# Seven block products in place of eight for the second layer's first product

## The chip, the cores and the metric

The kernel runs on one core of a Trainium2 chip. Times are device microseconds (us) of one execution. Engines go by their names in the profile: PE is TensorE's matmul stream and PEld its weight loads, DVE is VectorE, ACT is ScalarE, SP is SyncE, which here only issues DMAs. The program gives each engine its own list of instructions, in an order fixed when it is built.

## The reference

Sliding-window attention (4 sequences of 576 tokens, 8 heads of 64, window 64) gives x of 2304 tokens by 512. Two gated layers follow, each with a w_in of 512 by 2048 and a w_out of 2048 by 512:

```python
attn = softmax(where(mask, q @ k.T / 8, -1e9)); x = attn @ v      # 2304 x 512
h = x @ w_in1;  x = (h - tanh(h)) @ w_out1
h = x @ w_in2;  out = (h * sigmoid(1.702 * h)) @ w_out2
```

The four weights arrive as 64-bit floats and are converted on the chip.

## The kernel before

**Numbers.** Every operand of a large product is kept as two float32r tiles, a rounded high part and the rest (ACT copies `hi`, DVE subtracts `lo`). `three` (L540 to L545) makes one product of three matmuls: hi*hi, hi*lo, lo*hi. So a product of 128 by 128 weights with 512 tokens is three matmuls of 512 columns.

**Layers.** The 2048 hidden features are 16 groups f of 128. A step of a block of n tokens is `hid` (12 matmuls into one PSUM bank psh, 4 slices kk of the 512 inputs), then `act1` (ACT, L567 or L569), `act2` (DVE, L573), `act3` (ACT, L577), `act4` (DVE, L581), and two steps later `proj`, which adds to the accumulator banks acc. Layer 1 (blocks of 512, 512, 256, 512, 512 tokens) sends its result to DRAM (`xs`, L636), layer 2 (512, 512, 512, 512, 256) loads it back (`load_x2`). Blocks 0 and 1 of layer 1 are made in two parts each, which layer 2 adds (L664). The attention of tokens 1024 to 2303 runs in between layer 1's steps.

**Weights.** `plan_w` loads one group of 128 (512 KB), then ACT takes the absolute value (L275), four DVE operations form the 32-bit number (L279, L282, L288, L294), ACT rounds the high part (L301), DVE takes the rest (L306). A converted pair (w_in and w_out of one f) lives in one of 16 SBUF tiles, tags w0 to w15. Layer 2's pair f takes the tile of layer 1's pair f once that has had its last use (`last_proj[f]`).

**Order.** `Plan` is a list scheduler that runs when the program is built. Each task has the engines it may use with a planned time, a due time as its priority, what it comes after, and buffers that it takes (`acq`) and gives back (`rel`), out of fixed counts: raw=3, cw=2, s=4, psh=2, gp=3 and so on. It yields one order for PE, DVE, ACT and SP. PE's large products are chained in a fixed order. The planned times are constants, for instance 0.62 for a DVE operation on 512 elements and 0.36 on 256.

## Time and profile before

| what | value |
|---|---|
| median of 3 runs | 888.97 us (888.82 to 889.29) |
| profiled execution, its own time | 886.63 us |
| its span, first to last instruction | 884.8 us |
| mean granted TensorE clock | 0.994 of full |
| PE, PEld, DVE, ACT busy | 863.4, 725.9, 470.6, 374.7 us |
| DMA bytes | 72.93 MB |

The span is 1.83 us under the profiled execution's own time, and that time is 2.34 us under the median of the runs without a profile. Layer 2 begins at 482 us of the span.

### The profile page before, as it was taken

The numbers are of one execution on the slowest core, as the hardware profiler recorded it, in microseconds if no ns is written. First come the engines' busy times: TensorE is split into PE (matmuls) and PEld (weight loads), VectorE is DVE, ScalarE is ACT, GpSimd is POOL, SyncE is SP. The second block draws the span as 40 slices with busy tenths as digits, with TensorE's granted clock in tenths as the row PEclk, the third lists the DMA queues.
The fourth block names the chain that finished last, engine by engine and source line by source line (L and its number), as shares of the span: only waits on it lengthen the run. The fifth ranks groups of instructions, "written<-read, shape, count | busy, mean of one in ns | idle before, by whom it ended". The sixth has DMA issues, their size and how long they took to land.

```text
span 884.8 us, 13040 instructions
## 1 busy us (share of the span) xinstructions
PE 863.4 (98%) x5188; PEld 725.9 (82%) x5188; DVE 470.6 (53%) x867; ACT 374.7 (42%) x888; POOL 4.0 (0%) x19
## 2 busy tenths in 40 slices
PE   6799999999999999999999999999999999999998
PEld 5588888888899888878888888888888888888897
DVE  6899999233555325445999995233323332322232
ACT  6878565223546325543556653222222222222222
POOL 1000000000000000000000000000000000000000
PEclk8999999999999999999999999999999999999999
DMA  9645454111132102101554551020002000200000
GB/s 335 237 123 170 144 191 159 32 48 54 61 120 90 49 0 84 54 25 72 167 192 143 191 165 49 0 96 1 1 0 96 1 1 0 72 1 1 34 15 24
DMA packets 44205, 72.93 MB, mean 82 GB/s; under 512 B 3312, under 2 KB 24304, under 8 KB 44144
## 3 DMA queue, kind: packets, MB, share of 16 engines
q1 hardware_dynamic: 43712, 71.58, 24.1%
q8 instruction: 40, 0.66, 0.3%
q10 hardware_dynamic: 432, 0.52, 0.2%
q14 instruction: 21, 0.17, 0.1%
HBM read 60.56 MB, written 11.53 MB: 81 GB/s over the span
## 4 chain that ended last, share of the span: by engine, by line
PE 93%; DMA 2%; DVE 2%; ACT 1%; SPq 0%; issue 0%; ACTq 0%
PE acc L545 45%; PE psh L545 44%; PE psa L419 2%; PE psa L484 1%; PE psa L467 1%; DMA raw<-in_w_in 1%; ACT s L444 1%; DMA early<-in_k 1%; DMA early<-in_v 1%; DVE xl L504 0%; DVE nm L432 0%; DVE s L460 0%; DVE cw L288 0%; DVE w L306 0%; ACT s L472 0%
## 5 line engine op out<-in xcount | busy, mean ns | idle before, releaser
L545 PE MATMUL psh<-xh,w 128*128 128x512 f32 (+1 forms) x1312 | 391.3, 365 | 3.2 <-DVE g L573 2.5
L545 PEld LDWEIGHTS psh<-xh,w 128*128 128x128 f32 x1312 | 238.7, 189 | 44.1 <-DVE g L573 2.7
L573 DVE TENSOR_TENSOR g<-psh,g 128x512 f32<-128x512 f32 (+1 forms) x164 | 102.4, 624 | 286.8 <-ACT g L569 196.2
L545 PE MATMUL psh<-xl,w 128*128 128x512 f32 (+1 forms) x656 | 238.5, 364 | 0.2 <-DVE xl L504 0.2
L545 PE MATMUL acc<-gh,w 128*128 128x512 f32 (+1 forms) x672 | 198.4, 362 | 0.0
L545 PE MATMUL acc<-w,gh 128*128 128x512 f32 x576 | 190.3, 389 | 0.0
L545 PEld LDWEIGHTS psh<-xl,w 128*128 128x128 f32 x656 | 123.7, 189 | 20.0 <-DVE xl L504 0.5
L545 PEld LDWEIGHTS acc<-gh,w 128*128 128x128 f32 x672 | 122.1, 190 | 20.7 <-issue 1.5
L581 DVE TENSOR_TENSOR gl<-g,gh 128x512 fp32r<-128x512 f32 (+1 forms) x164 | 102.5, 625 | 66.3 <-ACT gh L577 65.0
L569 ACT ACTIVATE g<-psh 128x512 f32<-128x512 f32 (+1 forms) x80 | 44.5, 556 | 207.2 <-PE psh L545 207.0
L577 ACT ACTIVATE gh<-g 128x512 fp32r<-128x512 f32 (+1 forms) x164 | 95.4, 582 | 80.7 <-DVE g L573 80.5
L545 PEld LDWEIGHTS acc<-w,gh 128*128 128x128 f32 x576 | 108.2, 188 | 22.1
L545 PE MATMUL acc<-gl,w 128*128 128x512 f32 (+1 forms) x336 | 120.9, 360 | 0.0
L545 PE MATMUL acc<-w,gl 128*128 128x512 f32 x288 | 112.2, 390 | 0.0
L567 ACT ACTIVATE g<-psh 128x512 f32<-128x512 f32 (+1 forms) x84 | 45.0, 538 | 127.8 <-PE psh L545 127.8
L545 PEld LDWEIGHTS acc<-gl,w 128*128 128x128 f32 x336 | 63.8, 190 | 9.2
L545 PEld LDWEIGHTS acc<-w,gl 128*128 128x128 f32 x288 | 54.1, 188 | 10.7
L275 ACT ACTIVATE cw<-raw 128x512 f32<-128x512 f32 x64 | 43.6, 681 | 21.5 <-DVE w L306 17.0
L301 ACT ACTIVATE w<-cw 128x512 fp32r<-128x512 f32 x64 | 40.7, 637 | 24.7 <-DVE cw L294 24.4
L288 DVE SCALAR_TENSOR_TENSOR cw<-raw,cw 128x512 uint32<-128x512 uint32 x64 | 43.9, 686 | 1.0
L306 DVE TENSOR_TENSOR w<-cw,w 128x512 fp32r<-128x512 f32 x64 | 43.8, 684 | 0.7 <-ACT w L301 0.7
L294 DVE SCALAR_TENSOR_TENSOR cw<-raw,cw 128x512 uint32<-128x512 uint32 x64 | 43.8, 685 | 0.2
(58 smaller groups left out, 458.6 us busy)
## 6 DMA issues: line engine op xcount, KB each, us to landing
raw<-in_w_in SPq DMA_DIRECT2D x32, 512.0 KB, 3.7
raw<-in_w_out SPq DMA_DIRECT2D x32, 512.0 KB, 3.5
vt<-in_v SPq DMA_DIRECT2D x11, 512.0 KB, 3.6
xs<-os SPq DMA_DIRECT2D x20, 256.0 KB, 3.2
out<-os SPq DMA_DIRECT2D x16, 256.0 KB, 2.2
kt<-in_k SPq DMA_DIRECT2D x9, 384.0 KB, 4.1
qt<-in_q SPq DMA_DIRECT2D x11, 256.0 KB, 2.8
early<-in_v SPq DMA_DIRECT2D x5, 512.0 KB, 8.0
```

Source lines behind the costliest of these rows:

```text
L275: nc.scalar.activation(bits[key].bitcast(F32), raw[key].bitcast(F32)[:, :, 1], AF.Abs)
L288: nc.vector.scalar_tensor_tensor(out=bits[key], in0=raw[key][:, :, 0], scalar=29, in1=bits[key], op0=ALU.logical_shift_right, op1=ALU.bitw ...
L294: nc.vector.scalar_tensor_tensor(out=bits[key], in0=raw[key][:, :, 1], scalar=0xC0000000, in1=bits[key], op0=ALU.bitwise_and, op1=ALU.bitw ...
L301: nc.scalar.activation(wt[layer, f][:, i, 0, :], bits[key].bitcast(F32), AF.Copy)
L306: nc.vector.tensor_tensor(out=lo, in0=bits[key].bitcast(F32), in1=hi.bitcast(F32), op=ALU.subtract)
L419: nc.tensor.matmul(ps[h][part(j, h), p, :], lhsT=qt[j][r, p, :], rhs=kt[j][r, :, p, :], start=not on_pe, stop=not on_pe or p == NP - 1,)
L545: nc.tensor.matmul(ps, lhsT=a, rhs=b, start=first and i == 0, stop=last and i == 2)
L567: nc.scalar.activation(g, psh[s], AF.Tanh)
L569: nc.scalar.activation(g, psh[s], AF.Sigmoid, scale=BETA)
L573: nc.vector.tensor_tensor(out=g, in0=psh[s], in1=g, op=ALU.subtract if s[0][0] == 1 else ALU.mult)
L577: nc.scalar.activation(gh, g, AF.Copy)
L581: nc.vector.tensor_tensor(out=gl, in0=g, in1=gh.bitcast(F32), op=ALU.subtract)
```

## The change

Layer 2's blocks become one of 256 tokens (tokens 0 to 255, computed as before) and two units of 1024 tokens. In a unit, h is computed pair by pair: pair j holds the feature groups 2j and 2j+1. Both matrices are cut in two by two blocks (features by inputs: A11, A12, A21, A22, each 128 by 256; inputs by tokens: B11 and so on, each 256 by 512), and the four blocks of h come from seven products of 6 matmuls each (Winograd's form), with sums ahead and behind:

- `plan_wd` (8 times, among layer 1's steps, one for each pair): converts the two w_in groups, forms S1 to S4 on DVE, splits the eight blocks in hi and lo and stores them in DRAM (`wd`, 2 MiB for each pair).
- `stream`/`load_ws`: load a pair's blocks from `wd` into four tiles (tags w8 to w11, 1 MiB each): four blocks for the first 256 tokens, seven for a unit.
- w_out of layer 2 now lives two groups to a tile in w0 to w7 and is gated behind the last store of `wd`.
- `plan_xu`: loads the unit's x from `xs`, forms T1 to T4 on DVE and splits B11, T1, B22, T3, T2, B21, T4 in hi and lo, in two halves i that share their buffers (kq, v). T1, T3, B21, B22 of unit 0 take the tiles w12 to w15 after layer 1's `last_proj` of 12 to 15.
- `Ma`, `Mb`: four products, then three; between and behind them stand two `proj` fillers of 12 matmuls. DVE forms U, W, V, C22, C11, C12, C21 out of PSUM. The gated blocks of the first 512 tokens go to `proj` at once, those of the second 512 to DRAM (`u_store`) and come back (`u_back`) for 16 `proj` behind the eighth pair.
- `UB`: in unit 0 the products use the banks h, h, a0, a1 and the accumulators acc0 to acc3, in unit 1 the other way round.
- The kernel's last step is now a `proj` of two groups on four token tiles, each evicted in halves.

```diff
+    sizes = {1: [512, 512, 256, 512, 512], 2: [256]}
     blocks = {l: [(sum(z[:i]), n) for i, n in enumerate(z)] for l, z in sizes.items()}
-    NB1, NB2 = len(blocks[1]), len(blocks[2])
+    NB1 = len(blocks[1])
+    units = [256, 1280]
...
-    plan = Plan(dict(raw=3, cw=K["cw"], s=K["s"], psh=2, g=2, gp=3, kq=1, v=1, sa=K["sa"], x=2, acc0=1, acc1=1, acc2=1, acc3=1, a0=1, a1=1))
+    plan = Plan(dict(raw=3, cw=K["cw"], s=K["s"], psh=2, g=2, gp=3, kq=1, v=1, sa=K["sa"], x=2, acc0=1, acc1=1, acc2=1, acc3=1, a0=1, a1=1, ws=4))
...
+    A21, A11, A12, A22, S1, S2, S3, S4 = range(8)
+    HB = NB // 2
+    wd = {}
+    stage = {}
+    def blocks_of(j):
+        a, b = (bits[2, 2 * j + i, 0].bitcast(F32) for i in range(2))
...
+        for o, a, b, op in ((S1, A21, A22, ALU.add), (S2, S1, A11, ALU.subtract), (S3, A11, A21, ALU.subtract), (S4, A12, S2, ALU.subtract)):
+            nc.vector.tensor_tensor(out=x[o], in0=x[a], in1=x[b], op=op)
+    def wd_hi(j, i):
+        o = stage[j, i] = st.tile([P, NB], F32R, tag="s", name="wds")
+        nc.scalar.activation(o[:, :HB], blocks_of(j)[i], AF.Copy)
+    def wd_lo(j, i):
+        o = stage[j, i]
+        nc.vector.tensor_tensor(out=o[:, HB:], in0=blocks_of(j)[i], in1=o[:, :HB].bitcast(F32), op=ALU.subtract)
+    def wd_store(j, i):
+        if j not in wd:
+            wd[j] = dr.tile([P, 8, NB], F32, name=f"wd{j}")
+        nc.sync.dma_start(out=wd[j][:, i], in_=stage.pop((j, i)).bitcast(F32))
+    wd_done = {}
+    def plan_wd(j, d, after):
+        signs, ls, cs = [], [], []
+        both = add({"SP": 1.2}, lambda _: [load_w((2, 2 * j + i, 0)) for i in range(2)], d - 5, after, acq=("raw", "raw"), size=2 * P * NB * 8)
+        for i in range(2):
+            key = (2, 2 * j + i, 0)
+            def go(e, fn, t, *a, key=key, **kw):
+                return add({e: t}, lambda _: fn(key), d + 3 * i, *a, **kw)
+            l = both
+            c = absol = go("ACT", conv_abs, 0.56, [l] + cs, acq=() if i else ("cw", "cw"))
+            for fn, x in ((conv_clamp, 0.36), (conv_mant, 0.36), (conv_low, 0.62)):
+                c = go("DVE", fn, x, [c])
+            signs.append(go("DVE", conv_sign, 0.62, [c], rel=[("raw", l)] if i else []))
+            ls.append(l)
+            cs.append(absol)
+        sums = add({"DVE": 1.4}, lambda _: wd_sums(j), d + 6, signs)
+        los, sts = [], []
+        for i in range(8):
+            h = add({"ACT": 0.32}, lambda _, i=i: wd_hi(j, i), d + 6 + i, [sums], acq=("s",))
+            los.append(add({"DVE": 0.36}, lambda _, i=i: wd_lo(j, i), d + 6 + i, [h]))
+            sts.append(add({"SP": 0.6}, lambda _, i=i: wd_store(j, i), d + 6 + i, [los[-1]], rel=[("s", h)], size=P * NB * 4))
+        wd_done[j] = sts
+        add({"none": 0.0}, lambda _: None, d, los, rel=[("cw", cs[0]), ("cw", cs[0]), ("raw", ls[0])])
+        return sts[-1]
...
+    def load_ws(key, j, a, b):
+        n = count[0] = count[0] + 1
+        t = wp.tile([P, 4, NB], F32R, tag=f"w{8 + (n - 1) % NS}", name="ws")
+        wstream[key] = (t, a)
+        nc.sync.dma_start(out=t[:, : b - a].bitcast(F32), in_=wd[j][:, a:b])
...
+    UB = [(["h", "h", "a0", "a1"], ["acc0", "acc1", "acc2", "acc3"]), (["acc0", "acc1", "acc2", "acc3"], ["h", "h", "a0", "a1"])]
...
+    def load_u(u, what, i, kk, t0):
+        for c, b, z in pieces(t0, NB):
+            nc.sync.dma_start(out=full(u, what, i)[:, c], in_=xs[b, parts[b][0]][:, kk, z])
+    def load_u_more(u, what, i, kk, c, b, z, fa):
+        t = x2[u, what, i, b] = st.tile([P, NB], F32, tag="s", name="x2b")
+        nc.sync.dma_start(out=t[:, c], in_=xs[b, fa][:, kk, z])
...
+    def combine(u, o, a, b, op, i):
+        o, a, b = (full(u, w, i) for w in (o, a, b))
+        nc.vector.tensor_tensor(out=o, in0=a, in1=b, op=op)
...
+    def prod(u, j, n, a, b):
+        key = (1 + u, j, 0 if a < S2 else 1)
+        ah, al = ws_of(key, a)
+        bh, bl = x_space(u, b)
+        for i in range(2):
+            c = slice(i * P, (i + 1) * P)
+            three(mb[u, j, n], ah[:, c], al[:, c], bh[i], bl[i], i == 0, i == 1)
+    def m_open(u, j):
+        mb[u, j, 0] = bank(UB[u][0][0], "m")
+        prod(u, j, 0, A11, "B11")
+    def m_first(u, j):
+        for n, a, b in ((1, S2, "T2"), (2, S1, "T1"), (3, S3, "T3")):
+            mb[u, j, n] = bank(UB[u][0][n], "m")
+            prod(u, j, n, a, b)
+    def m_more(u, j, n, a, b):
+        mb[u, j, n] = bank(UB[u][0][n], "m")
+        prod(u, j, n, a, b)
...
+    def u_one(u, j):
+        r = cv.tile([P, 2, NB], F32, tag="raw", name="uv")
+        ut[u, j, 0], ut[u, j, 1] = r[:, 0], r[:, 1]
+        nc.scalar.activation(ut[u, j, 0], mb[u, j, 0], AF.Copy)
+    def u_add(u, j, o, a, n):
+        if o == "W":
+            ut[u, j, 2] = st.tile([P, NB], F32, tag="cw", name="c12", bufs=K["cw"])
+        if o == "C22":
+            ut[u, j, 3] = st.tile([P, NB], F32, tag="s", name="c22")
+        nc.vector.tensor_tensor(out=u_val(u, j, o), in0=u_val(u, j, a), in1=mb[u, j, n], op=ALU.add)
...
+    def u_proj(u, t, fs, es):
+        for e in es:
+            if fs[0] == 0:
+                uacc[u, t, e] = bank(UB[u][1 - t][e], "uacc")
+            for f in fs:
+                wh, wl = w_outof(2, f)
+                _, gh, gl = ug[u, t, f]
+                c = slice(e * P, (e + 1) * P)
+                three(uacc[u, t, e], wh, wl, gh[:, c], gl[:, c], f == 0, f == KF - 1, swap=True)
...
+        if what == "h" and layer == 2:
+            plan_w((2, f, 1), due["p", s] - 6, [last_proj[f // 2]], wd_done[NJ - 1])
+            if f % 2 == 0:
+                j = f // 2
+                stream((0, j), j, 0, 4, d)
...
+    def stream(key, j, a, b, d):
+        n = len(streams)
+        last = list(streams.values())[-1:]
+        after = wd_done[j] + last + ([last_proj[8 + n]] if n < NS else [])
+        streams[key] = add({"SP": 0.6}, lambda _: load_ws(key, j, a, b), d - 14, after, acq=("ws",), size=P * (b - a) * NB * 4)
...
+    for what, s in seq:
+        layer, f = s[0][0], s[1]
+        if layer == 2 and not wd_done:
+            last = None
+            for j in range(NJ):
+                d = K["wd"][0] + K["wd"][1] * j
+                near = [made[x] for x in made if due["h", x] < d - 8]
+                last = plan_wd(j, d + K["wd"][2], near[-1:] + [last])
+        if layer == 1 or what == "h" or f < KF - 2:
+            plan_step(what, s)
...
+    def plan_xu(u, d, ends_of, gate):
+        done = []
+        t4own = xown = last = None
+        for i in range(2):
+            srcs = {}
+            acq, before = ("kq", "v"), [last]
+            lfirst = None
+            for n, (what, kk, t) in enumerate((("B11", i, 0), ("B12", i, 1), ("B22", 2 + i, 1), ("B21", 2 + i, 0))):
+                dd = d - 30 + 12 * i + 2 * n
+                t0 = units[u] + t * NB
+                deps = [stored[z, kk] for c, b, _ in pieces(t0, NB) for z in turns if z[:2] == (1, b)]
+                near = [made[s] for s in made if due["h", s] < dd - K["xu"]]
+                np_ = len(list(pieces(t0, NB)))
+                c = l = add(
+                    {"SP": 0.6 * np_}, lambda _, a=(u, what, i, kk, t0): load_u(*a), dd - 6,
+                    deps + near[-1:] + gate + [lfirst], acq=() if lfirst else acq, size=P * NB * 4,
+                )
+                lfirst = lfirst or l
+                for sl, b, z in pieces(t0, NB):
+                    for fa in parts[b][1:]:
+                        m = add({"SP": 0.6}, lambda _, a=(u, what, i, kk, sl, b, z, fa): load_u_more(*a), dd - 5.9, [l], acq=("s",), size=P * NB * 2)
+                        c = add({"DVE": 0.36}, lambda _, a=(u, what, i, sl, b): add_u(*a), dd, [c, m], rel=[("s", m)])
+                srcs[what] = c
+            dd = d - 20 + 12 * i
+            los = {}
+            def split(what, *w, acq=(), i=i, dd=dd, los=los):
+                h = add({"ACT": 0.54}, lambda _: u_hi(u, what, i), dd, list(w) + ends_of(what), acq=acq)
+                los[what] = add({"DVE": 0.62}, lambda _: u_lo(u, what, i), dd, [h])
+                return h
+            def comb(o, x, y, op, *w, i=i, dd=dd):
+                return add({"DVE": 0.62}, lambda _: combine(u, o, x, y, op, i), dd, list(w))
+            h = split("B11", srcs["B11"], xown, acq=("x",) if i == 0 else ())
+            xown = xown or h
+            t1 = comb("T1", "B12", "B11", ALU.subtract, srcs["B12"], srcs["B11"])
+            split("T1", t1)
+            t3 = comb("T3", "B22", "T3", ALU.subtract, srcs["B22"], t1)
+            split("B22", srcs["B22"])
+            split("T3", t3)
+            t2 = comb("T2", "T3", "T2", ALU.add, t3, t1, los["B11"])
+            split("T2", t2)
+            split("B21", srcs["B21"])
+            t4 = comb("T4", "T4", "T2", ALU.subtract, t2, los["B21"])
+            h = split("T4", t4, t4own, acq=("sa", "sa") if i == 0 else ())
+            t4own = t4own or h
+            last = add({"none": 0.0}, lambda _: None, dd, list(los.values()), rel=[("kq", lfirst), ("v", lfirst)])
+            done += los.values()
+        return done, xown, t4own
...
+    rest = [("p0", s) for s in last_p0]
+    order = []
+    for u in range(2):
+        for j in range(NJ):
+            order += [("Ma", u, j), rest.pop(0) if rest else None, ("Mb", u, j), rest.pop(0) if rest else None]
+            rest += [("p", u, 0, (2 * j + i,)) for i in range(2)]
+        q_ = [("p", u, 1, (f,)) for f in range(KF)]
+        order += [rest.pop(0), q_[0], rest.pop(0)]
+        if u == 0:
+            order += q_[1 : KF - 2]
+            rest = q_[KF - 2 :]
+        else:
+            order += q_[1 : KF - 2] + [("p", u, 1, (KF - 2, KF - 1))]
+    order = [o for o in order if o]
...
+    had = {0: lambda w: [last_proj[KF - 4 + ("T1", "T3", "B21", "B22").index(w)]] if w in ("T1", "T3", "B21", "B22") else []}
...
+            stream((1 + u, j, 0), j, 1, 5, d)
+            stream((1 + u, j, 1), j, 5, 8, d)
+            mk = keys(UB[u][0])
+            a0 = prev = add({"PE": MS}, lambda _, u=u, j=j: m_open(u, j), d, [prev, streams[1 + u, j, 0]] + (xdone if j == 0 else []), acq=mk[:1])
+            a1 = prev = add({"PE": 3 * MS}, lambda _, u=u, j=j: m_first(u, j), d + MS, [prev, streams[1 + u, j, 1]], acq=mk[1:])
+            chain += [a0, a1]
+            def sm(o_, a, n, *w, u=u, j=j, d=d, **kw):
+                return add({"DVE": 0.7}, lambda _: u_add(u, j, o_, a, n), d + 4, list(w), **kw)
+            p1 = add({"ACT": 0.52}, lambda _, u=u, j=j: u_one(u, j), d + 2, [a0], acq=("raw",))
+            uu = sm("U", "P1", 1, p1, a1, rel=[(mk[1], a1)])
+            ww = sm("W", "U", 2, uu, acq=("cw",))
+            vv = sm("V", "U", 3, ww)
+            c22 = sm("C22", "W", 3, ww, vv, acq=("s",))
+            up[u, j] = (a0, a1, p1, uu, ww, vv, c22, mk)
...
+            for n, a, x, w in ((0, A12, "B21", [p1]), (2, S4, "B22", [ww]), (3, A22, "T4", [vv, c22])):
+                rel = [("ws", streams[1 + u, j, i]) for i in ((1,) if n == 2 else (0,) if n == 3 else ())]
+                if end and n == 3:
+                    rel += [("x", uo[u][0]), ("sa", uo[u][1]), ("sa", uo[u][1])]
+                b = prev = add({"PE": MS}, lambda _, a=(u, j, n, a, x): m_more(*a), d, [prev] + w, rel=rel)
+                ms.append(b)
+                chain.append(b)
+            if end:
+                gone[u] = b
...
+            y22 = act("C22", c22, d)
+            c11 = sm("C11", "P1", 0, d + 3, a0, uu, ms[0])
+            y11 = act("C11", c11, d + 3)
+            c12 = sm("C12", "W", 2, d + 3.5, a1, c22, ms[1])
+            c21 = sm("C21", "V", 3, d + 3.6, a1, c22, ms[2])
+            y21 = act("C21", c21, d + 4)
+            y12 = act("C12", c12, d + 5)
+            s22 = add({"SP": 0.6}, lambda _, u=u, j=j: u_store(u, j, "C22"), d + 5, [y22], rel=[("s", c22)], size=P * NB * 4)
+            s12 = add({"SP": 0.6}, lambda _, u=u, j=j: u_store(u, j, "C12"), d + 5, [y12], rel=[("cw", ww)], size=P * NB * 4)
+            store_of[u, 2 * j], store_of[u, 2 * j + 1] = s12, s22
+            los = []
+            for f, y in ((2 * j, y11), (2 * j + 1, y21)):
+                h = add({"ACT": 0.54}, lambda _, u=u, f=f: g_hi(u, 0, f), d + 5, [y], acq=("gp",))
+                gates[u, 0, f] = add({"DVE": 0.62}, lambda _, u=u, f=f: g_lo(u, 0, f), d + 5, [h])
+                los.append(gates[u, 0, f])
+                owner[u, 0, f] = h
...
+                    bk = add({"SP": 0.6}, lambda _, u=u, f=f: u_back(u, f), d - 9, [store_of[u, f]] + chain[-6:-5], acq=("raw",), size=P * NB * 4)
+                    h = add({"ACT": 0.54}, lambda _, u=u, f=f: g_hi(u, 1, f), d - 4, [bk] + (chain[-3 + i : -2 + i or None] if f > 1 else [gates[u, 0, KF - 2 + f]]), acq=("gp",))
+                    gates[u, 1, f] = add({"DVE": 0.62}, lambda _, u=u, f=f: g_lo(u, 1, f), d - 4, [h], rel=[("raw", bk)])
+                    owner[u, 1, f] = h
...
+            es = [[0], [1, 2, 3]] if fs[0] == 0 else [[0], [1], [2], [3]] if final else [[0, 1, 2, 3]]
+            for z in es:
+                last_e = z[-1] == 3
+                p = prev = add(
+                    {"PE": MS / 2 * len(z) * len(fs)}, lambda _, a=(u, t_, fs, z): u_proj(*a), d, [prev] + need,
+                    acq=[bk_[e] for e in z] if fs[0] == 0 else (), rel=[("gp", owner[u, t_, f]) for f in fs] if last_e else (),
+                )
```

## Rows read from the trace of the kernel before

**Rows 1.** The page's first part: busy us, share of the span, instructions.
```profile
PE 863.4 (98%) x5188; PEld 725.9 (82%) x5188; DVE 470.6 (53%) x867; ACT 374.7 (42%) x888; POOL 4.0 (0%) x19
```
**Rows 2.** The waits of PE, 100 to 840 us: total, times, longest.
```profile
PE psh L545 <- ACT xh L499: 0.7, 1, 0.7
PE psa L484 <- DVE s L474: 0.3, 1, 0.3
PE psh L545 <- DVE xl L504: 0.2, 1, 0.2
```
**Rows 3.** The chain that ended last, layer 2's first steps: start, us, what.
```profile
482.13 2.72 PE psh L545 x12
484.85 2.72 PE acc L545 x12
```
**Rows 4.** The same chain at the end of the kernel (256-token steps, tail).
```profile
873.92 1.39 PE acc L545 x6
875.31 1.43 PE psh L545 x12
876.75 4.12 PE acc L545 x18
```
**Rows 5.** Groups by form: busy us, mean ns of one, idle before.
```profile
L545 PEld LDWEIGHTS psh<-xh,w 128*128 128x128 f32 x1312 | 238.7, 189 | 44.1 <-DVE g L573 2.7 <-issue 1.0 <-ACT xh L499 0.8
L573 DVE TENSOR_TENSOR g<-psh,g 128x512 f32<-128x512 f32 x124 | 85.7, 691 | 249.0 <-ACT g L569 171.0 <-ACT g L567 77.3
L577 ACT ACTIVATE gh<-g 128x512 fp32r<-128x512 f32 x124 | 78.4, 632 | 68.4 <-DVE g L573 68.2
L288 DVE SCALAR_TENSOR_TENSOR cw<-raw,cw 128x512 uint32<-128x512 uint32 x64 | 43.9, 686 | 1.0
L294 DVE SCALAR_TENSOR_TENSOR cw<-raw,cw 128x512 uint32<-128x512 uint32 x64 | 43.8, 685 | 0.2
L306 DVE TENSOR_TENSOR w<-cw,w 128x512 fp32r<-128x512 f32 x64 | 43.8, 684 | 0.7 <-ACT w L301 0.7
L275 ACT ACTIVATE cw<-raw 128x512 f32<-128x512 f32 x64 | 43.6, 681 | 21.5 <-DVE w L306 17.0 <-DMA raw<-in_w_in 2.9 <-ACT gh L577 0.8
L569 ACT ACTIVATE g<-psh 128x512 f32<-128x512 f32 x64 | 38.3, 598 | 180.7 <-PE psh L545 180.6
L282 DVE TENSOR_SCALAR cw<-cw 128x512 uint32<-128x512 uint32 x64 | 26.9, 422 | 0.4
L577 ACT ACTIVATE gh<-g 128x256 fp32r<-128x256 f32 x40 | 17.0, 426 | 12.3 <-DVE g L573 12.3
L581 DVE TENSOR_TENSOR gl<-g,gh 128x256 fp32r<-128x256 f32 x40 | 16.9, 422 | 13.2 <-ACT gh L577 12.7 <-PE acc L545 0.5
```
**Rows 6.** Stretches: PE, PEld, DVE, ACT, POOL busy (instructions), clock, DMA share, GB/s.
```profile
160.00:200.00 40.00, 40.00 (x179) 33.10 (x177) 11.69 (x18) 10.22 (x17) 0.00 (x0) 1.00 0.08 27
200.00:240.00 40.00, 40.00 (x303) 32.94 (x302) 17.24 (x30) 17.42 (x55) 0.00 (x0) 1.00 0.17 60
240.00:295.00 55.00, 55.00 (x604) 52.79 (x603) 29.07 (x61) 29.58 (x102) 0.00 (x0) 1.00 0.30 97
295.00:345.00 50.00, 50.00 (x290) 41.51 (x289) 17.48 (x29) 17.39 (x42) 0.00 (x0) 1.00 0.08 24
345.00:395.00 50.00, 48.67 (x383) 38.92 (x381) 24.78 (x42) 25.14 (x80) 0.00 (x0) 1.00 0.19 59
395.00:406.00 11.00, 11.00 (x48) 9.12 (x49) 2.71 (x5) 3.12 (x6) 0.00 (x0) 1.00 0.00 1
406.00:482.00 76.00, 76.00 (x337) 62.90 (x337) 69.25 (x128) 41.03 (x69) 0.00 (x0) 1.00 0.47 159
...
571.00:837.00 266.00, 266.00 (x1186) 220.70 (x1186) 77.52 (x117) 68.73 (x118) 0.00 (x0) 1.00 0.07 22
```
**Rows 7.** Stretches of the kernel's first part, same columns.
```profile
60.00:80.00 20.00, 17.93 (x249) 15.50 (x248) 18.76 (x43) 15.08 (x57) 0.00 (x0) 1.00 0.54 176
100.00:150.00 50.00, 50.00 (x222) 41.39 (x222) 48.85 (x92) 29.72 (x49) 0.00 (x0) 1.00 0.51 170
```
**Rows 8.** L279 (a conversion's first DVE step) alone, 395 to 482 us.
```profile
395.00:482.00 87.00, 7.49 (x18) 1.00 0.41 139
```
**Rows 9.** DMA issues: KB each, median us to landing.
```profile
xs<-os SPq DMA_DIRECT2D x20, 256.0 KB, 3.2
x<-xs SPq DMA_DIRECT2D x8, 256.0 KB, 4.0
x2b<-xs SPq DMA_DIRECT2D x8, 256.0 KB, 4.3
```
**Rows 10.** The first 20 us of the span, columns as in rows 6.
```profile
0.00:20.00 20.00, 12.98 (x164) 9.74 (x166) 13.44 (x33) 13.19 (x49) 4.00 (x19) 0.87 0.94 327
```

More of the change, by code (lines that the diff above doesn't have):

```diff
@@ L107, in order @@
                     for k, owner in t["rel"]:
-                        at(end + self.HOP, "back", (k, owner["own"][k]))
+                        at(end + self.HOP, "back", (k, owner["own"][k].pop(0)))
                     for o in t["outs"]:
@@ L145 @@
     fill=0.75,
+    xu=34.0,
+    wd=(190.0, 25.0, 60.0),
     seg=(4, 7),
@@ L590, in proj @@
         _, gh, gl = gt.pop(s)
-        wh, wl = (wt[layer, f][:, 1, j, :] for j in range(2))
+        wh, wl = w_outof(layer, f)
         n = c1 - c0
@@ new lines, in attn_moe2_kernel, with full @@
+    xtmp = {}
+    IN_PLACE = dict(B12="T3", B11="T2", B21="T4")
+    def full(u, what, i):
+        if (u, i) not in xtmp:
+            k_, v_ = (ap_.tile([P, 2, NB], F32, tag=t, name="xt", bufs=1) for t in "kv")
+            q_ = ap_.tile([P, NB], F32, tag="q", name="xt", bufs=1)
+            xtmp[u, i] = dict(T2=k_[:, 0], T3=k_[:, 1], T1=v_[:, 0], B22=v_[:, 1], T4=q_)
+        return xtmp[u, i][IN_PLACE.get(what, what)]
+    def load_u(u, what, i, kk, t0):
+        for c, b, z in pieces(t0, NB):
+            nc.sync.dma_start(out=full(u, what, i)[:, c], in_=xs[b, parts[b][0]][:, kk, z])
@@ L770, in attn_moe2_kernel, with plan_step @@
     x2_planned = set()
-    w2_planned = set()
-    for what, s in seq:
+    chain = []
+    def plan_step(what, s):
+        nonlocal prev
         z, f = s
@@ L779, in attn_moe2_kernel @@
             plan_x2(bi, d)
-        if layer == 2 and (f, 0) not in w2_planned:
-            for i in range(2):
-                w2_planned.add((f, i))
-                plan_w((2, f, i), due["hp"[i], s] - 6, [last_proj[f]])
+        if what == "h" and layer == 2:
[3 more added lines that the diff above has]
+                stream((0, j), j, 0, 4, d)
         if what == "h":
```

235 lines of the change are left out of this document (196 added, 39 removed).

## The prediction

> **What bounds the kernel now.** I read the page's busy times first. PE is busy 98% of the span, DVE 53%, ACT 42% [rows 1]. Since an average can hide a stage with another limit, the next view is PE's waits behind the first 100 us: three waits, 1.2 us in all, up to 840 us [rows 2]. The idle PE time left over lies in the first 80 us and in the tail, which the change doesn't touch. Third is the chain of waits in layer 2: it is matmuls alone, `hid` and `proj` in turn, each 2.72 us for 12 matmuls of 512 columns [rows 3], so one matmul costs 2.72/12 = 0.2267 us. That this is the pace of the matmuls and not of what feeds them shows in two rows: a weight load lasts 0.189 us [rows 5], less than 0.2267, and with half the columns 12 matmuls of `hid` take 1.43 us, 0.119 each, with a weight load for each as before [rows 4]. Hence every matmul taken out of layer 2 gives back 0.2267 us, as long as what replaces it stays under PE.
>
> **What is removed.** Before, four blocks of 512 tokens take 4 x 16 x 12 = 768 matmuls of `hid`. After, two units take 2 x 8 pairs x 7 products x 6 = 672. The difference is 96, that is 8 groups of 12: 8 x 2.72 = 21.76 us. `proj` keeps its number (768 and 96), and the 256-token block only moves from the end to the front of layer 2. A product ends after 6 matmuls and then changes its bank; `proj` in layer 2 changes banks after every 3 and still takes 2.72 us for 12 [rows 3], so that costs nothing.
> [...]
>
> **Added in layer 1: the weights' sums.** `plan_wd` puts 8 bursts into the stretch in which layer 1's `hid` are due at 182 to 357 us (190 + 25 j, less 8); in the trace that begins near 160, and the bursts can run on to 395, where layer 1's last block starts. By the durations of rows 5, one burst costs DVE 2 x (0.422 + 0.422 + 0.686 + 0.685) = 4.43 us for two conversions, 4 sums and 8 remainders of 256 elements at 0.422 = 5.06, together 9.5 us; eight cost 76 us. From 160 to 395 us DVE is busy 11.69 + 17.24 + 29.07 + 17.48 + 24.78 = 100.3 of 235 us [rows 6], so 134.7 are free: it fits, and DVE goes to 75%. ACT gets 2 x 0.681 + 8 x 0.426 = 4.8 us a burst, 38 in all, beside 99.8. DMA gets 8 x (1.05 MB in + 2.10 MB out) = 25 MB over 235 us, 107 GB/s on top of 24 to 97 [rows 6]; the first 20 us moved 327 [rows 10].
> What fitting doesn't exclude: in a burst DVE is full, and the planner counts 3.92 + 1.4 + 2.88 = 8.2 us for what lasts 9.5. DVE can so fall 1.3 us behind the planned order in each burst, and PE, whose list also holds the transposes and products of the attention, waits for it there. Behind a late DVE operation stand ACT's exponentials or copies, and then that PE group and all of layer 1 behind it. Bounds: 0, and 8 x 1.3 = 10.4 us. Two rows frame it: with DVE full and attention running, PE lost 2.07 of 20 us (60 to 80); with DVE as full and no attention, nothing (100 to 150) [rows 7]. The bursts carry a due time 60 us later than their place, so attention's steps pass them in the planner's queue, and lateness dies out when DVE has a pause. I take a quarter: 2.6 us.
> A second thing: `wd`'s stores hold the four `s` buffers that layer 1's evictions also want. A buffer is held for 0.43 + 0.42 us and 3.2 us of store [rows 5, 9], so with all four taken one comes back each 1.0 us; four evictions get theirs within 4.05 us and end 0.69 later, at 4.74. The fourth bank is wanted after one `hid` and three quarters of a `proj`, 2.72 + 2.04 = 4.76. So nothing, at worst one landing, 3.2 us, at each of three block ends: 0 to 9.6, I take 0, since evictions have the earlier due time.
>
> **Moved: w_out's conversion.** Before, 18 of 32 conversions of layer 2 begin between 395 and 482 us [rows 8], 18 x (2.215 + 0.684) = 52 us of the 72 us of DVE there [rows 6]. Now 16 stand there (46 us), which may start as soon as w0 to w7 are free, in the first half of that stretch. 87 - 20 - 46 = 21 us of DVE stay free, so all are ready when layer 2 starts. Behind 482 us the rest of the 32 is gone. Cost 0. Its loads stand on SP behind the last store of `wd`; that is due some 50 us earlier.
>
> **Added at the start of layer 2: unit 0's sums of x.** The cover is the 256-token block: 14 steps of 1.43 + 1.39 = 2.82 us, two more `hid`, and layer 1's last two `proj`, 14 x 2.82 + 2.86 + 5.44 = 47.8 us, so the first product is wanted at about 530 us. DVE has 12 additions of parts at 0.422 and 8 sums and 14 remainders at 0.69, 20.2 us, beside 13.4 us of the block's own gates. The first half can end only after layer 1's last `proj` frees w15, at about 491; say 495. The second half then loads over shared buffers (4.0 and 4.3 us [rows 9]), at 503, and has 10 us of DVE at some two thirds of the engine: 518. Margin 12 us; cost 0. Without that cover it would be the whole second half, 23 us. Unit 1's sums (17.7 of DVE, nothing to add) lie under some 17 `proj` of 2.72, 46 us; cost 0.
>
> **Added in each pair.** PE's cycle is 42 + 24 = 66 matmuls, 14.96 us. DVE: 7 sums, 4 gates, 2 remainders, 13 x 0.69 = 9.0 us. ACT: a copy and two roundings at 0.63, four sigmoids at 0.60, 4.3 us. The tightest wait: `Ma` ends at 5.44, then U, W, V, C22 take 4 x 0.69 plus small gaps, to some 8.5; W is wanted at 9.52 and C22 at 10.88, since a filler of 2.72 and one product stand between. Margin 2 us, cost 0; with 0.5 us of wait a pair it would be 8. The accumulators go to `proj` a full `Ma` later. DMA: 1.84 MB of blocks and 0.52 MB of stores in 14.96 us, 158 GB/s, which is what 406 to 482 us already shows (159 at a share of 0.47 [rows 6]); two of four tiles are filled while two are read, a lead of a whole pair. SP issues 4 DMAs a pair; a store that waits for its gates holds up the next block's load by a few us, inside that lead. The second phase has one rounding, one remainder and one load for each 2.72 us; cost 0. ACT's functions are those of before.
> **The tail.** It ends as before with half evictions and a store; the last matmul group ends at 880.87 and the span at 884.8 [rows 4]: 3.9 us, kept.
>
> **Sum.** -21.76 + 2.6 = -19.2 us. On the profiled execution 886.63 becomes 867.5 (span 884.8 to 865.6). The median shown is 2.34 us above that execution; carried over, 888.97 becomes 869.8 us.
>
> **Rivals.**
> *A, forecast (0.72):* waits of 0 to 6 us, 867 to 873.5.
> *B, the bursts cost in full (0.12):* 10.4 us of lateness in layer 1, or its like at the evictions. For it: PE lost 10% in 60 to 80 [rows 7]. Against: DVE at 75%, not 95%. 888.97 - 21.76 + 10.4 = 877.6, 874 to 882.
> *C, the blocks' loads set the pace (0.06, the slower side):* a pair needs 2.36 MB. If DMA gives less than 2.36/14.96 = 158 GB/s, PE waits in each of 16 pairs; at 2.36 MB/(14.96 + 1.36) = 145 GB/s the whole gain is gone. At 130 GB/s a pair takes 18.2 us: 16 x 3.2 = 51 us lost, 918. For it: one queue, which in layer 2 moved only 22 GB/s for 266 us [rows 6]. Against: 159 at half a share, 327 in the first 20 us [rows 6, 10].
> *D, a matmul is worth less when removed (0.02):* were the feeding the limit, the smallest pace seen is 0.119 [rows 4]: 96 x 0.119 = 11.4 us, 877.5. Against: rows 3 and 5. [...]
> *E, unit 0's x is late (0.08):* 12 us more than I reckon uses up the margin, each further us is lost; up to 23 us, 872 to 892, a third of it within 0.2% of before.
>
> **How the numbers follow.** 0.2% (1.8 us) is about what a measurement of this kernel can tell from no change. Faster: A, B, D and 0.05 of E, 0.91; the same: 0.03 of E; slower: C, 0.06. The range takes A without its edges and those parts of B, D and E that lie under 878: 866.2 to 878, 0.8. Its lower end is the full 21.76 and 1 us for the small waits of before.
>
> **What the profile after would show.** PE busy about 842 us; the chain in the units still matmuls, 12 in 2.72 us; the seven products as 672 matmuls. DVE at 75% from 160 to 395 us, low behind 482 us but for the sums of x. PE's new waits, if A or B holds, for DVE in the attention of 170 to 395 us. DMA bytes about 145 MB, near 160 GB/s in the pairs. Wrong, if PE waits on a DMA into a weight tile (C), stands still at about 530 us (E), or if the units' matmuls come closer than 0.2267 us (D).

## The result and the profile after

The changed kernel takes 864.3 us (median of 4 runs, 863.94 to 864.9), the kernel before beside it 888.89 us (4 runs, 887.12 to 889.29): ratio 0.9728, 95% interval 0.9711 to 0.9745. It is faster, as forecast, but lies 1.9 us under the low end of the range, 866.2. The profiled execution takes 863.94 us, its span 862.1; before, 886.63 and 884.8. One execution of a kernel below (the extra sums as three tasks) took 1207.69 us at a mean granted clock of 0.653, where all others have 0.94 or more, and is left out.

Busy times of the page, to set beside [rows 1]:
```profile
PE 841.4 (98%) x5092; PEld 707.7 (82%) x5092; DVE 577.4 (67%) x1090; ACT 403.7 (47%) x971; POOL 4.0 (0%) x19
```
PE has 96 matmuls fewer and is 22.0 us less busy; DVE has 107 us more to do. PE's waits from 100 us to the end, beside [rows 2]:
```profile
PE psh L653 <- ACT xh L607: 0.7, 1, 0.7
PE psa L592 <- ACT s L580: 0.2, 1, 0.2
PE psh L653 <- DVE xl L612: 0.2, 1, 0.2
PE psa L592 <- DVE s L582: 0.2, 1, 0.2
```
They add up to 1.3 us, before to 1.2, and none of them is in layer 2. The chain that ended last, one pair of unit 0 (m are the seven products, uacc is `proj`), beside [rows 3]:
```profile
571.65 5.44 PE m L653 x24
577.09 2.72 PE uacc L653 x12
579.81 4.08 PE m L653 x18
583.89 2.72 PE uacc L653 x12
```
66 matmuls in 14.96 us, 0.2267 us each, without a gap. Where the 22.7 us of span went can be read from three marks. The first full-width steps start at 76.64 us before and 76.17 after. Layer 2 starts at 482.13 [rows 3] and 481.65. The last matmul group ends at 880.87 [rows 4] and at 858.62:
```profile
849.99 8.63 PE uacc L653 x38
...
858.64 0.44 DVE os L929
```
So the first 80 us gave 0.47 (less than they vary by from one execution to the next, as the first two experiments show), the rest of layer 1 nothing, layer 2 went from 398.74 to 376.97, that is 21.77, and the tail behind the last matmul from 3.9 to 3.5 us. The 96 matmuls were reckoned at 21.76.

Stretches, columns as in [rows 6]; the first five answer to the first five there:
```profile
160.00:200.00 40.00, 40.00 (x178) 33.11 (x178) 26.52 (x55) 16.84 (x36) 0.00 (x0) 1.00 0.40 138
200.00:240.00 40.00, 40.00 (x303) 32.92 (x302) 24.89 (x50) 21.94 (x68) 0.00 (x0) 1.00 0.58 183
240.00:295.00 55.00, 55.00 (x605) 52.78 (x604) 41.95 (x95) 36.01 (x119) 0.00 (x0) 1.00 0.54 174
295.00:345.00 50.00, 50.00 (x290) 41.52 (x289) 33.12 (x68) 25.08 (x64) 0.00 (x0) 1.00 0.42 141
345.00:395.00 50.00, 48.63 (x383) 38.93 (x382) 33.11 (x65) 30.14 (x95) 0.00 (x0) 1.00 0.58 185
...
571.00:700.00 129.00, 129.00 (x570) 106.83 (x569) 72.24 (x112) 41.67 (x70) 0.00 (x0) 1.00 0.49 166
```
From 160 to 395 us DVE is busy 159.6 of 235 us, 68%; the prediction said 75%. Why the bursts are shorter than reckoned shows in one of them, DVE in order of time (start, us, line):
```profile
307.82 0.42 DVE L297 TENSOR_SCALAR cw<-cw 128x512 f32<-128x512 f32 x1
308.27 0.43 DVE L300 TENSOR_SCALAR cw<-cw 128x512 uint32<-128x512 uint32 x1
308.62 0.42 DVE L297 TENSOR_SCALAR cw<-cw 128x512 f32<-128x512 f32 x1
308.95 0.69 DVE L306 SCALAR_TENSOR_TENSOR cw<-raw,cw 128x512 uint32<-128x512 uint32 x1
309.55 0.42 DVE L300 TENSOR_SCALAR cw<-cw 128x512 uint32<-128x512 uint32 x1
309.89 0.69 DVE L312 SCALAR_TENSOR_TENSOR cw<-raw,cw 128x512 uint32<-128x512 uint32 x1
310.49 0.68 DVE L306 SCALAR_TENSOR_TENSOR cw<-raw,cw 128x512 uint32<-128x512 uint32 x1
311.26 0.69 DVE L679 TENSOR_TENSOR g<-psh,g 128x512 f32<-128x512 f32 x1
311.87 0.68 DVE L312 SCALAR_TENSOR_TENSOR cw<-raw,cw 128x512 uint32<-128x512 uint32 x1
312.59 0.43 DVE L362 TENSOR_TENSOR raw<-cw 128x256 f32<-128x256 f32 x1
313.05 0.42 DVE L362 TENSOR_TENSOR raw<-raw,cw 128x256 f32<-128x256 f32 x1
313.39 0.42 DVE L362 TENSOR_TENSOR raw<-cw 128x256 f32<-128x256 f32 x1
313.73 0.42 DVE L362 TENSOR_TENSOR raw<-cw,raw 128x256 f32<-128x256 f32 x1
314.06 0.69 DVE L687 TENSOR_TENSOR gl<-g,gh 128x512 fp32r<-128x512 f32 x1
314.67 1.43 DVE L370 TENSOR_TENSOR wds<-cw,wds 128x256 fp32r<-128x256 f32 x4
```
An operation of 512 elements lasts 0.69 us, but the next one mostly starts 0.60 behind it; one of 256 (or of the cheap kind on 512) lasts 0.42 and is followed after 0.34. So in this full queue an operation costs the spacing, 0.60 or 0.34 us, and not the duration, 0.69 or 0.42. By these spacings a burst takes 2 x (0.34 + 0.34 + 0.60 + 0.60) + 12 x 0.34 = 7.8 us of DVE. In the burst shown it is some 8.3, without the gate's operations (g, gl) in between, since a few steps start later, 0.45 behind an operation of 0.42 and 0.72 behind one of 0.68. The planner had counted 8.2 us, with 0.62 and 0.36 for one operation, close to these spacings. So there was next to no lateness to pay for.

### The profile page after: what moved, and what is told of

It reads as the page before. It is cut to its first block, busy times and chain, and to the rows that moved or that the text cites. A ratio compares the mean times of both kernels' runs of the same rounds, so it can differ in the third digit from the quotient of the medians.

```text
span 862.1 us, 13640 instructions
## 1 busy us (share of the span) xinstructions
PE 841.4 (98%) x5092; PEld 707.7 (82%) x5092; DVE 577.4 (67%) x1090; ACT 403.7 (47%) x971; POOL 4.0 (0%) x19
## 2 busy tenths in 40 slices
DMA packets 69842, 144.29 MB, mean 167 GB/s; under 512 B 6160, under 2 KB 29712, under 8 KB 66704
## 4 chain that ended last, share of the span: by engine, by line
PE 94%; DVE 3%; ACT 2%; DMA 1%; issue 0%; ACTq 0%
PE acc L653 26%; PE psh L653 25%; PE uacc L653 20%; PE m L653 18%; PE psa L592 2%; PE psa L575 2%; PE psa L527 1%; ACT s L552 1%; DVE nm L540 1%; DMA raw<-in_w_in 1%; DVE xl L612 0%; DVE s L582 0%; DVE w L328 0%; DVE s L568 0%; DVE cw L306 0%
## 5 line engine op out<-in xcount | busy, mean ns | idle before, releaser
L653 PE MATMUL psh<-xh,w 128*128 128x512 f32 (+1 forms) x672 | 197.6, 362 | 3.2 <-DVE g L679 2.5
L653 PE MATMUL uacc<-w,gh 128*128 128x512 f32 x512 | 162.5, 389 | 0.0
L653 PEld LDWEIGHTS psh<-xh,w 128*128 128x128 f32 x672 | 121.6, 189 | 23.2 <-DVE g L679 2.7
L653 PE MATMUL psh<-xl,w 128*128 128x512 f32 (+1 forms) x336 | 120.8, 359 | 0.2 <-DVE xl L612 0.2
L653 PEld LDWEIGHTS uacc<-w,gh 128*128 128x128 f32 x512 | 96.1, 188 | 20.0
L653 PE MATMUL uacc<-w,gl 128*128 128x512 f32 x256 | 99.6, 389 | 0.0
L653 PE MATMUL m<-xu,ws 128*128 128x512 f32 x384 | 92.2, 389 | 0.0
L653 PEld LDWEIGHTS m<-xu,ws 128*128 128x128 f32 x384 | 72.1, 188 | 14.9
L653 PEld LDWEIGHTS psh<-xl,w 128*128 128x128 f32 x336 | 63.5, 189 | 9.5 <-DVE xl L612 0.5
L653 PEld LDWEIGHTS uacc<-w,gl 128*128 128x128 f32 x256 | 48.1, 188 | 9.9
L293 ACT ACTIVATE cw<-raw 128x512 f32<-128x512 f32 x64 | 42.2, 673 | 15.2 <-DVE w L328 10.8
```

The source lines that it names most:

```text
L293: nc.scalar.activation(bits[key].bitcast(F32), raw[key].bitcast(F32)[:, :, 1], AF.Abs)
L653: nc.tensor.matmul(ps, lhsT=a, rhs=b, start=first and i == 0, stop=last and i == 2)
```

## The experiments

Times of both kernels vary by some 3 us with the clock at the start (886.69 to 889.97 us and 863.94 to 867.04, in the result and the first two experiments below), so a loss in layer 1 is also read from the traces: the start of each tanh against the same one in the changed kernel's trace, from behind the start (about 80 us) to the end of layer 1.

**The kernel before, against itself.** No edit.

> The kernel before, unchanged, against itself. Two readings of the 1.6 us by which the changed kernel came in under its range. Theory 1: the profiled execution of before (886.63) and the other runs (887.12 to 889.29) are draws of one kernel whose start varies by some 2 us from execution to execution; then these runs scatter over 886.6 to 889.3, the ratio is 1.000, and a profile of a long one shows the extra time in the first 80 us, with the matmuls' pace of 2.72 us for 12 behind it. Theory 2: a run without a profile is always some 2 us longer than the profiled one; then all runs lie at 888.8 to 889.3 and only the profiled one near 886.6.

Ratio 0.9999 (0.9988 to 1.001). Of its 12 runs the five with a mean clock of 0.994 take 886.69 to 887.76 us, the seven with 0.988 to 0.990 take 888.27 to 889.97. The profile was again one of the short ones (span 884.9). That is theory 1: the runs scatter, and two others without a profile came as low as 886.69 and 886.93.

**The changed kernel, again.** No edit.

> The changed kernel, unchanged. Theory (the scatter of 2 to 3 us is the clock of the first 50 us, drawn anew in each execution): its runs scatter over 863.9 to 867, those with the higher mean clock at the low end, and the lowest run lies 21.8 to 23 us under the lowest of the kernel before on the same chip. Rival (the changed kernel has really lost the scatter and gained some 2.3 us by it): all its runs within 863.9 to 865, and the medians 24 us or more apart.

866.2 us (864.74 to 867.04), ratio 0.9752 (0.9739 to 0.9766) to 888.27 beside it. The run with a clock of 0.993 takes 864.74, those with 0.987 to 0.989 take 866.2 to 867.04. That is the theory, not the rival; the lowest runs of both kernels on this chip, 864.74 and 886.68, lie 21.9 apart. So the first four runs of the changed kernel had all drawn the short start (clock 0.993), and three of the four of before, by their times, a longer one. Like beside like, from these two experiments and the first result (several chips): at 0.993 to 0.994 the medians are 886.93 (5 runs) and 864.58 (5 runs), 22.4 us apart; at 0.987 to 0.990 they are 889.43 (7) and 866.2 (3), 23.2 apart. The mean clock sorts the runs only roughly: two runs of before on this chip took 888.17 and 888.35 us at 0.994.

**Eight products again.** One product of each pair is computed twice.
```diff
     def m_more(u, j, n, a, b):
...
         prod(u, j, n, a, b)
+        if n == 0:
+            prod(u, j, n, a, b)
```


> The changed kernel with one product of each pair computed twice, so eight products of 6 matmuls as before the change; sums, stores, streams and order of the new scheme all stay. Theory (the gain is the 96 matmuls and nothing else): 16 x 1.36 = 21.8 us over the changed kernel, 885.9 to 886.5, and a span within 1 us of before. Rival (the new order of layer 2 or the moved block brings something of its own): it stays clearly under that, 884 or less. Rival (the additions cost something that the shorter PE work now uncovers): above 888.

886.62 us (886.1 to 889.1), ratio 0.9987 (0.9976 to 0.9999), span 884.8, the same as before's. The six runs with a clock of 0.994 take 886.1 to 886.62. Its layer 2 lasts from 482.56 to 881.29 us, 398.73, where before had 398.74. The gain is the 96 matmuls, and some 0.5 us beside them, about what the shorter tail gives; everything that was added lies under PE.

**The planner told longer durations for a burst.**
```diff
-            for fn, x in ((conv_clamp, 0.36), (conv_mant, 0.36), (conv_low, 0.62)):
+            for fn, x in ((conv_clamp, 0.42), (conv_mant, 0.42), (conv_low, 0.69)):
...
-        sums = add({"DVE": 1.4}, lambda _: wd_sums(j), d + 6, signs)
+        sums = add({"DVE": 1.7}, lambda _: wd_sums(j), d + 6, signs)
```
The last DVE step of a conversion goes from 0.62 to 0.69 as well, and the eight splits from 0.32 and 0.36 to 0.42.

> The changed kernel, with the planner told the measured durations of a burst of weight sums (0.42 and 0.69 us in place of 0.36 and 0.62, 1.7 in place of 1.4 for the four sums). The prediction's term of 2.6 us says that lateness of DVE against the planned order makes PE wait in layer 1. If some of that is left in the changed kernel, this one gains up to 2 us. If the term is nothing, within 0.5 us of the changed kernel's 864.3.

866.61 us (866.12 to 868.77). Neither reading came: there is no gain, and it isn't within 0.5 us either. At a clock of 0.994 it takes 866.12 to 866.61, and by its trace layer 1 loses 1.5 us, 1.4 of them in one wait of an attention step for DVE. The profiled execution shows the long start. The stretch from 20 to 40 us, first in the changed kernel, then here:
```profile
20.00:40.00 20.00, 15.78 (x190) 12.72 (x190) 16.59 (x40) 15.23 (x63) 0.00 (x0) 0.93 0.73 278
```
```profile
20.00:40.00 20.00, 16.59 (x182) 13.28 (x182) 15.38 (x37) 14.10 (x61) 0.00 (x0) 0.76 0.74 283
```
Up to 80 us the same instructions stand in the same order on PE, DVE and ACT in both; the granted clock is 0.93 and 0.76, and the first full-width step starts at 76.17 and at 79.45 us. Behind that both kernels go on at 2.72 us for 12.

**More work in the bursts.** The four sums are done four times, and in a second kernel twice (12 and 4 more DVE operations of 256 elements a burst), untold to the planner; a third tells it 6.5 us for the sums of the four times. In the diff `...` stands for the rest of a line:
```diff
-        for o, a, b, op in ((S1, A21, A22, ALU.add), ... ):
+        for o, a, b, op in 3 * ((S1, A21, A22, ALU.add), ... ) + ((S1, A21, A22, ALU.add), ... ):
```


> The changed kernel with the four weight sums of each burst done four times (12 more DVE operations of 256 elements, 5.1 us a burst, 40 us in all), which the planner is not told. Theory (DVE's free time in 160 to 395 us, 75 us, takes it, and lateness dies out): PE busy throughout, 864 to 866. Rival (lateness goes to PE through attention's steps, as the prediction's term had it): a quarter of 40 us, 10 us more, 874; in full, 904.

> The changed kernel with the four weight sums of each burst done twice (4 more DVE operations, 1.7 us a burst, 13.5 us in all), untold to the planner: DVE then falls 3.0 us behind the plan in a burst, where the changed kernel falls 1.3 and the run with four times the sums 6.3. Theory: layer 1 swallows a lateness up to some microseconds, since attention's PE groups are planned with that much room; then 864 to 866. Rival: PE pays in proportion, a third of what the run with four times the sums lost in layer 1 (13.8 us by its trace): 869.

> The same extra work as in the run with four times the sums (5.1 us a burst, 40 us of DVE), but the planner is told it (6.5 us for the sums). Theory (lateness against the planned order is what PE pays for, not DVE's load): most of the 15 us comes back, 864 to 870. Rival (DVE's load itself does it, 75 us free minus 40): it stays at 876 to 880.

Four times: 879.28 us (876.27 to 880.81), ratio 0.9885 (0.9864 to 0.9905); layer 1 loses 13.8 us. Twice: 866.05 (865.52 to 867.64), 0.6 us. Four times and told: 881.22 (878.78 to 881.88), ratio 0.9917 (0.9901 to 0.9933), 14.0 us. By the spacing above the extra work is 4.1 and 1.4 us a burst and not 5.1 and 1.7.

Twice the sums is the test of the prediction's term. By the spacings a burst then takes 9.2 to 9.7 us against 8.2 in the plan, so DVE falls 1.0 to 1.5 us behind in each, about the 1.3 that the prediction feared, and layer 1 loses 0.6 us in all. That is nearer to none of it than to a quarter.

With four times the sums and the planner untold, layer 1 loses its 13.8 us in five steps of 1 to 5 us. In the chain at each of them stands the unbroken piece of sixteen sums, 5.9 us, ahead of attention's steps. Here is part of it in the largest, 5.0 us:
```profile
258.35 1.44 DVE raw L362 x4
...
262.75 1.10 DVE raw L362 x3
...
264.37 0.69 DVE s L568
...
265.19 1.07 PE psa L575 x8
```
Told of it, the planner only moves the loss: 4.7 us near 245 us and 9.3 at the start of layer 1's last block. PE's longest waits were for attention:
```profile
PE psa L575 <- ACT s L566: 7.6, 2, 6.2
```
The last attention tile shows how. In the changed kernel its scores (`L527`) start on PE at 380.8 us, and three groups of 12 matmuls run before its next step at 390.2. Here the sixteen sums stand on DVE from 386.6 to 392.2 us, ahead of the step that ends the tile before (xl, 392.5); the scores follow at 396.9, behind the last matmuls that could have covered them, and PE waits:
```profile
396.99 1.10 PE psa L527 x32
...
404.23 1.94 PE psa L575 x8
...
406.84 2.00 PE psa L592 x32
...
409.51 5.07 PE psh L653 x12
```
The last line holds a second price: behind the pause 12 matmuls take 5.07 us in place of 2.72, begun at a granted clock of 0.50 (see the last section). Telling the planner brought nothing back, so the theory that lateness against the plan is what PE pays for fell; the long piece on DVE cost in either order, 13.8 and 14.0 us.

**The same work in smaller pieces.** The extra sums as three tasks of 1.7 us behind the first, then as twelve of 0.42.
```diff
         sums = add({"DVE": 1.4}, lambda _: wd_sums(j), d + 6, signs)
+        for _ in range(3):
+            sums = add({"DVE": 1.7}, lambda _: wd_sums(j), d + 6, [sums])
```


> The same 40 us of extra weight sums as in the runs with four times the sums, told to the planner, but as three more tasks of 1.7 us behind the first in each burst, so that attention's steps can pass between them. Theory (what cost layer 1 some 14 us in both of those runs is the unbroken piece of 6.8 us on DVE, which stands in front of a gate or an attention step): 864 to 869. Rival (DVE's load, and the buffers that a longer burst holds): 876 to 881 as before.

> The same 40 us of extra weight sums once more, told to the planner as twelve single operations of 0.42 us behind the four in each burst, so that no piece on DVE is longer than in the changed kernel. If the unbroken piece alone cost layer 1 its 14 us (a third of it was left with pieces of 1.7 us, 868.8 to 871.5), this one lies at 864 to 867 and its trace has no new wait of PE between 160 and 480 us. If the load or the longer held buffers cost the rest, it stays at 868 to 872, with new waits for attention's steps there.

Three tasks: 868.82 to 871.48 us in four runs, 4 to 5 us over the changed kernel at a like clock; there is no trace to say where. Twelve tasks: 876.61 (875.6 to 877.97), ratio 0.987 (0.9853 to 0.9886); layer 1 loses 10.2 us. The last burst runs from 393.7 us on, across the start of the last block: 3.0 us are lost there, with its conversion on DVE ahead of the last tile's xl, and 7.2 at the evictions of the block before. The chain there:
```profile
410.08 0.62 ACT wds L371 x2
...
412.56 2.69 DMA wd<-wds
...
415.42 1.02 ACT wds L371 x3
...
416.60 2.35 DMA wd<-wds
...
419.04 0.70 DVE os L736
...
419.78 3.58 PE acc L660 x9
```
The eviction (os, L736) waits for a store of weight sums to give back its `s` buffer, and PE waits for the evicted bank: the second price that the prediction put at 0 and bounded at 3.2 us for each block end. SP has all eight stores of the burst ahead of the block's own. So smaller pieces take away the loss of the long piece, at least in part, and bring another: the burst lasts longer and meets the end of a block.

**The bursts moved, no work added.** First 25 us later, then 25 us earlier.
```diff
-    wd=(190.0, 25.0, 60.0),
+    wd=(215.0, 25.0, 60.0),
```


> The changed kernel with its eight bursts of weight sums set 25 us later (215 + 25 j), no work added. The last burst's stores then leave at about 411 in place of 386 us, across the last attention tile, the start of the last block of layer 1 at 395 and the evictions of the block before it at 400 to 410. Theory (what costs is a burst at that place, where its stores hold the s buffers and its operations stand ahead of evictions and attention): layer 1 loses 4 to 12 us there, 868 to 876. Rival (only added work or long pieces cost): 864 to 867.

> The changed kernel with its eight bursts 25 us earlier (165 + 25 j), no work added: the first ones then meet the end of layer 1's weight conversion, where DVE is full to 150 us, and the last ends some 25 us before the last block. Theory (place decides, and this place is free): 864 to 867 and no new wait of PE between 160 and 480 us. Rival (any move of the bursts disturbs attention as much): 868 or more.

865.65 us (864.76 to 866.84) and 866.16 (864.93 to 866.6); at a clock of 0.993 to 0.994 the lowest are 864.76 and 864.93. Layer 1 loses 0.3 us and nothing. The later bursts end at 414.9 us, across the block end at 400 to 410, and still PE doesn't wait there: the trace shows four stores of sums, then the four of the evicted block, then four of sums. So the theory of the first of the two fell and that of the second held: the place alone doesn't decide, and the change's own bursts are free at all three places.

**Twice the DMA.**
```diff
         nc.sync.dma_start(out=t[:, : b - a].bitcast(F32), in_=wd[j][:, a:b])
+        scr = dr.tile([P, 4, NB], F32, name=f"scr{n}")
+        nc.sync.dma_start(out=scr[:, : b - a], in_=wd[j][:, a:b])
```


> The changed kernel in which each load of weight blocks is followed by a copy of the same blocks from DRAM to a second place in DRAM, so that the queue moves some 36.7 MB more (in the pairs 1.84 MB more read and written again, past 280 GB/s on average). Theory (the blocks' loads have a lead of a pair, and DMA is half used): 864 to 868. Rival C of the prediction (DMA close to setting the pace): PE waits on the weight tiles in every pair, 880 and more.

874.18 us (872.21 to 876.91), ratio 0.9846 (0.9824 to 0.9868): 8 to 10 us lost, not the 864 to 868 of the theory, nor rival C's waits in every pair. Two stretches:
```profile
482.00:530.00 48.00, 44.41 (x265) 39.26 (x265) 27.08 (x59) 18.85 (x42) 0.00 (x0) 0.96 0.90 322
530.00:700.00 170.00, 167.84 (x744) 138.75 (x743) 98.55 (x155) 55.97 (x97) 0.00 (x0) 0.99 0.74 272
```
The first product of unit 0 starts at 536.43 us in place of 529.49, of which 1.0 comes from the start: DMA is at a share of 0.90 there, a copy of 1 MiB takes 12.55 us, and an addition of parts of x waits on DVE for its load until 514.25 us with the 256-token block's own gates behind it. The pairs themselves lose nothing: from 536 to 649 us PE is busy throughout at 291 GB/s, and a pair keeps its 14.96 us. The other 4.3 us are lost behind unit 0's last pair, where unit 1's x is loaded (10.93 us for one load) and its sums stand ahead of that pair's last gates.

**A longer DVE chain in each pair.**
```diff
-        nc.vector.tensor_tensor(out=u_val(u, j, o), in0=u_val(u, j, a), in1=mb[u, j, n], op=ALU.add)
+        for _ in range(9 if o == "C22" else 1):
+            nc.vector.tensor_tensor(out=u_val(u, j, o), in0=u_val(u, j, a), in1=mb[u, j, n], op=ALU.add)
```


> The changed kernel with the sum C22 of each pair written nine times over (8 more DVE operations of 0.69, 4.9 to 5.5 us between C22's inputs and the third product of Mb that waits for it). By the trace of the changed kernel C22 ends 4.1 us before that product starts, so PE waits some 0.8 to 1.4 us a pair: 13 to 22 us more, 877 to 887. By the prediction's margin of 2 us: 2.9 to 3.5 a pair, 910 to 920. If C22 is not what comes next, 864.

903.7 us (903.68 to 905.81), ratio 1.0182 (1.0164 to 1.02). PE's longest wait:
```profile
PE m L653 <- DVE c L885: 28.8, 16, 3.1
```
16 waits, one in each pair, 1.8 us on average. The eight repeats, which write the same tile, follow each other after 0.72 us (in the chain each is a link of 0.70, with 0.02 of issue): 5.8 us. In the changed kernel C22 ends at 578.41 us and the product that waits for it starts at 582.53, a margin of 4.1; 5.8 - 4.1 = 1.7. So that wait comes next in the pairs. The whole loss is 38.8 us by the spans when the start's 1.05 is taken off. The 28.8 of these waits and 2.2 of others are part of it; behind a wait the next six matmuls take 1.66 us in place of 1.36, some 4.8 us over the 16 pairs; 3.0 are left open.

**More filling at the start.** `fill=1.0` in place of 0.75.

> The changed kernel with the idle stretches that the planner sees in the first 90 us filled to 1.0 of their length with matmuls that only keep TensorE busy, in place of 0.75. If the scatter of the start comes from the clock falling behind such pauses, the runs move to the low end, 862 to 864.5, with a mean clock of 0.994 or more. Rival (the fill itself holds up the next useful matmul): 865 to 869.

866.16 us (864.95 to 867.48), clocks 0.987 to 0.993. The theory fell; the scatter stays, and nothing is gained. None of the runs points to a version that beats the changed kernel.

## Why the prediction was wrong, point by point

- *What bounds, and what is removed:* right. 21.76 us were reckoned, 21.77 are gone from layer 2's stretch, and putting an eighth product back returns that stretch to 398.73 us.
- *"I take a quarter: 2.6 us":* the step that failed first; layer 1 lost nothing. It rests on "8.2 us for what lasts 9.5", a sum of single durations. The operations of a burst follow each other at 0.60 and 0.34 us, and it takes 7.8 to 8.3 us of DVE. For matmuls the prediction had used the spacing, for DVE it used the mean of one. The quarter was too much as well: with twice the sums, which do put DVE that far behind, layer 1 lost 0.6 us. This step alone would have left 867.2, inside the range.
- *"carried over, 888.97 becomes 869.8":* the second one, and the one that put the time outside the range. The 2.34 us between the profiled execution and the median was taken for a fixed offset. It goes with the clock at the start, which comes out anew in each execution (a mean of 0.994 in the runs of before that took 886.69 to 887.76 us, 0.988 to 0.990 in those of 888.27 to 889.97): the median of before came from long starts, the four runs of after were all short ones. On the profiled executions alone the forecast was 867.5 against 863.94, 3.6 us: 2.6 from the first step, 0.5 at the start and 0.45 in the tail. The range's low end of 866.2 was the full gain taken from the longer median, so short starts were left out of it. As a gain that end is 22.8 us, and like beside like 22.4 to 23.2 were gained: which starts were drawn decided by how much the range was missed.
- *The s buffers, 0:* right here, but 3.2 us for a block end was no safe bound: with more work in the bursts an eviction did wait for a store, 4.5 us for one bank, and 7.2 us were lost at that block end.
- *w_out's conversion, 0:* right; no wait at the start of layer 2.
- *Unit 0's sums of x:* cost 0 right, margin mis-sized. The two halves' last remainders start here:
```profile
498.12 0.69 DVE L844 TENSOR_TENSOR t<-xt,t 128x512 fp32r<-128x512 f32 x1
...
523.50 0.69 DVE L844 TENSOR_TENSOR t<-xt,t 128x512 fp32r<-128x512 f32 x1
```
So they end at 499 and 524 us, where 495 and 518 were reckoned, and the first product starts at 529.49: 5 us of margin, not 12. The second half's loads ran past 510 us, with weight streams and stores ahead of them on SP. Unit 1's sums, put at 17.7 us, are 22 operations of 0.69, 15.2, as many as its trace has; nothing hangs on it.
- *The pairs:* cost 0 right; margin 4.1 us and not 2, since U starts when its own product is done and not at the end of `Ma`.
- *DMA:* 144.29 MB (145 reckoned) and 166 GB/s from 571 to 700 us; 175 in unit 0's pairs and 141 in unit 1's (158 reckoned). Rival C doesn't hold even at 291 GB/s; what twice the DMA hurt were the stretches in which a unit's x is loaded. Rivals B, D and E didn't come.
- *Left open:* why 33 us more of DVE work in the bursts cost 4 to 14 us in every form. Each trace shows its places: the unbroken piece ahead of attention's steps, in the planner's order or not, or, in small pieces, a longer burst that meets a block's end. A shortage of DVE time is not it: with four times the sums and the planner untold, DVE is busy 184 of 235 us from 160 to 395 us, and 173 and 170 in the run that was told and in the one with twelve tasks, so 51 us and more stay free. Why the planner, told of the work, finds no order that uses them is open, and so is where the run with three tasks loses.

## What to carry to other kernels

In the full stretches of DVE here an operation cost the distance to the next one's start (0.60 and 0.34 us, where one lasts 0.69 and 0.42), so read that from the order in time, for DVE as for matmuls, before a difference to a plan is made into a stall. PE was busy 98% with 1.2 us of waits from 100 us on, and the work taken from it came back in full (21.77 us of the 21.76 reckoned), since the added work kept its margins; price such margins one by one, and adding work to one suspect at a time shows which comes next. Free time on an engine doesn't say that a long piece on it is free (with 51 of 235 us free on DVE, unbroken pieces of 5.9 us cost 13.8 us): ask what stands behind it in that engine's order, and count a pause of PE with the slower matmuls behind it (5.07 us for 12 in place of 2.72, behind a wait of 6.2). When a profiled execution and the median differ, ask first whether runs scatter between two levels, and compare like with like.
